# One DMA queue, a new order of the first chunks' transfers, and weight conversions spread anew in a fused RWKV-7 and GELU MLP kernel

## The chip, the cores and the metric

The kernel runs on one core of one Trainium2 chip. A core has five engines with queues of their own: TensorE (PE, with its weight loads shown apart as PEld), VectorE (DVE), ScalarE (ACT), GpSimd (POOL) and SyncE (SP), which here only issues transfers. Each engine works through its instructions in order and waits on semaphores for the others. The metric is device time in microseconds (us), the median of several runs.

## The reference, cut to what matters

A recurrence over 768 steps runs for 4 batches of 8 heads with a 40 x 40 state; its output, seen as 3072 tokens of 320 values, goes through an MLP with an exact GELU. The two weights arrive as 64-bit floats (an array of `float32` times a numpy scalar of 64 bits), so a kernel has to make 32-bit floats of them.

```python
for t in range(S):                                  # S = 768
    y[:, :, t] = np.einsum('bhd,bhde->bhe', rt, state)
    Sa = np.einsum('bhde,bhe->bhd', state, at)
    state_decay = state * wt[:, :, None, :] - np.einsum('bhd,bhe->bhde', Sa, bt)
    state = state_decay + np.einsum('bhd,bhe->bhde', vt, kt)
x = y.transpose(0, 2, 1, 3).reshape(3072, 320)
h = x @ w_in                                        # 320 x 2048
g = 0.5 * h * (1.0 + erf(h * inv_sqrt2))
out = g @ w_out                                     # 2048 x 320
```

## The kernel before

The 768 steps are cut into 12 chunks of 64. In a chunk the recurrence becomes matrix products: with the running products of the decay w (`logs`, `sums`), b, k and a are scaled (`scale_b`, `scale_k`, `scale_a`) and flipped (`turn_*`); masked products of them give N, A, RV and M. The triangular system with N is inverted in blocks of 32 by 31 column steps on VectorE or GpSimd. N goes to HBM and comes back spread over partitions for that, and the inverse takes the same way back. Its corner is joined by products on TensorE (`corner`, `joined`: J). From it come `sa`, then QY, the outputs and the next state. The MLP of a chunk is cut into eight pieces, which `fill()` puts between the steps of later chunks: four make `ph` and the Gelu, four make `po`.

Chunks 0, 1 and 2 and the conversion of both weights are written out one after the other; the later chunks run in a loop. The parts that matter here, with cuts:

```python
    def rows_of ... / def fetch(c, n, src, eng, t=None):   # two transfers of 64 x 16 x 40
        ...
    def scale_k(c, eng=nc.gpsimd):
        rwv, _ = decays.pop(c)
        ks = turned_in[c]["ks"] = ks_ring()
        eng.tensor_tensor(ks[:, :, :, :D], raws.pop((c, "k")), rwv, ALU.mult)

    def to_float(dst, words, eng):                  # one piece: 64-bit words to 32-bit floats
        ...
        nc.vector.tensor_scalar(power, hi, 0x7FF00000, None, ALU.bitwise_and)
        nc.scalar.activation(power, power, ACT.Relu, bias=rebias, scale=8.0)
        nc.vector.tensor_scalar(mant, hi, 0x000FFFFF, 0x00100000, ALU.bitwise_and, ALU.bitwise_or)
        if eng is nc.vector:
            yield                                   # the rest comes with the next piece
        nc.vector.scalar_tensor_tensor(power, hi, 0x80000000, power, ALU.bitwise_and, ALU.bitwise_or)
        if eng is nc.vector:
            eng.scalar_tensor_tensor(mant_f, lo, 2.0 ** -32, mant, ALU.mult, ALU.add)
            eng.scalar_tensor_tensor(dst, mant_f, 2.0 ** -20, power_f, ALU.mult, ALU.mult)
        else:                                       # GpSimd: two products on ScalarE, then
            nc.scalar.mul(lo_f, lo, 2.0 ** -52)
            nc.scalar.mul(mant_f, mant, 2.0 ** -20)
            eng.tensor_tensor(mant_f, mant_f, lo_f, ALU.add)
            eng.tensor_tensor(dst, mant_f, power_f, ALU.mult)
        yield

    def convert(n, last=False):                     # begin n pieces, end the one begun before each
        for _ in range(n):
            begun.append(queue.pop(0)); next(begun[-1], None)
            if len(begun) > 1: next(begun.pop(0), None)
        if last:
            while begun: next(begun.pop(0), None)

    def first_load(last, part, at=None): ...        # part of w_in, four transfers (eight if last)
    def second_load(f, slot, at=late_raw): ...      # row block f of w_out, into a slot of raw words
    def seconds(n, *loads, last=False):             # convert(n), then these second_loads

    def store_inverse(c, engs=(nc.sync,)): ...      # 2 transfers; engs takes turns
    def fetch_inverse(c, engs=(nc.sync,)): ...      # 6 transfers, into Tt and T2
```

The raw words of the second weight lie in the tile that takes the result and in one spare tile, so a load into a slot waits until the block that was there has been read. The written-out part, cut to the steps that the change touches:

```python
    load_w(0); fetch(0, "b", ...); load_a(0); load_w(1, early_w); fetch(1, "b", ...); load_a(1, early_a)
    fetch(0, "k", k, nc.sync)
    fetch(1, "k", k, nc.sync, ahead["k"])
    # ... N of chunk 0 and 1, inverse of chunk 0 on VectorE, of chunk 1 on GpSimd
    load_VR(0); load_r(0); load_w(2)
    first_load(False, 0, early(0, 4)); first_load(False, 1)
    # ... products of chunk 0
    run(inverse)
    queues = nc.sync, nc.scalar
    store_inverse(0, queues); load_VR(1)
    first_pieces((0,), 0, nc.vector); convert(1)
    fetch_inverse(0, queues)
    mask_A(0); mask_RV(0); make_av(0); make_A(1, False)
    # ... joined(0) to outputs(0), the same of chunk 1, the rest of the first weight
    second_pieces(range(NF), nc.vector)             # NF = 16
    seconds(2); fill(); turn_k(2); seconds(1); fill()
    make_QY(1); outputs(1); pieces.append(mlp(1))
    turn_v(2); turn_r(2); make_RV(2); make_A(2)
    load_w(3); load_kb(3); load_VR(3); load_a(3)
    seconds(6); fill(); seconds(0, (10, 12))
    make_av(2); logs(3); sums(3); scale(3)
    # ... seconds(1), (1), (2), (1), (2) with the loads of blocks 11 to 15 between
    for c in range(2, NCH): ...                     # the loop
```

Of the kernel before, what the change touches and what calls it, by code (L numbers as in the profile page):

```python
# [12 lines left out]
ALU = mybir.AluOpType  # L13
# [6 lines left out]
def kernel(  # L20
# [119 lines left out]
    def fetch(c, n, src, eng, t=None):  # L140
        if t is None:
            t = work.tile([P, G, H, D], FP32, tag=n + "_raw", name=n + "_raw")
        for e in range(2):
            eng.dma_start(out=t[half(e)].rearrange("p g h d -> p (g h) d")[:, :, :D], in_=rows_of(src, c, e))
        raws[c, n] = t
# [24 lines left out]
    def load_w(c, t=None, eng=nc.sync):  # L170
        t = w_tile if t is None else t
        fetch(c, "w", w, eng, t[:, :G * DM].rearrange("p (g h d) -> p g h d", g=G, h=H))
        raws[c, "w"] = t
# [14 lines left out]
    def load_VR(c):  # L188
        VR = turned_in.setdefault(c, {})["VR"] = VR_ring()
        for e in range(2):  # L190
            nc.sync.dma_start(out=VR[half(e)].rearrange("p g q m d -> p (g q m) d")[:, :, :D], in_=rows_of(v, c, e))
# [34 lines left out]
    load_w(1, early_w)  # L226
    fetch(1, "b", b, nc.sync, ahead["b"])
    load_a(1, early_a)
    fetch(0, "k", k, nc.sync)
    fetch(1, "k", k, nc.sync, ahead["k"])  # L230
    for t in (paired["a"], early_a):
        nc.gpsimd.memset(by_64(t)[:, :, D:], 0.0)

# [75 lines left out]
    def convert(n, last=False):  # L309

        for _ in range(n):
            begun.append(queue.pop(0))
            next(begun[-1], None)
            if len(begun) > 1:
                next(begun.pop(0), None)
        if last:
            while begun:
                next(begun.pop(0), None)
# [56 lines left out]
    def first_pieces(kts, part, eng):  # L375
        queue.extend(first_convert(kt, part, eng) for kt in kts)
# [4 lines left out]
    def run(steps):  # L381
        for _ in steps:
            pass
# [4 lines left out]
    def logs(c):  # L388
        logw = raws[c, "w"][:, :G * DM]
        nc.scalar.activation(logw, logw, ACT.Ln)  # L390
# [43 lines left out]
    def scale_b(c):  # L434
        rwv, wp = decays[c]
        nb = nb_ring()
        nc.vector.scalar_tensor_tensor(nb[:, :, :, :D], raws.pop((c, "b")), -1.0, rwv, ALU.mult, ALU.mult)
        turned_in.setdefault(c, {}).update(nb=nb, wp=wp)
# [5 lines that stand above are left out]
# [29 lines left out]
    def turn_k(c):  # L473
        t = turned_in[c]
        kT = side("kT", "kT", 1)
        nc.scalar.copy(kT, flip(by_pair(t["ks"]), "kT_ps"))  # L476
        t["kT"] = parts(kT)
# [93 lines left out]
    def make_av(c):  # L571
        t = turned_in[c]
        av = duo("av")[:, :, :G * NP * D].rearrange("p x (g i d) -> p x g i d", g=G, i=NP)
        for g, i, x, e, q, m in units():
            mm(av[half(e ^ x), x, g, i], t["A"][half(e), x, g, i], t["VR"][half(e), g, q, m, :D])
        avs = t["avs"] = avs_ring()
        nc.scalar.copy(avs[:, :, :DM], av.rearrange("p x g i d -> p x (g i d)"))
# [4 lines left out]
    def start_inverse(c, eng, place=None):  # L582

        n = P // 2
        blk = blocks.pop(c).rearrange("j z n s t -> (j z n) s t")
        if place is None:
            Nb = work.tile([P, BL * BL], FP32, tag="Nb", name="Nb")
            W = work.tile([P, BL // 2 * BL], FP32, tag="W", name="W")
            tmp = work.tile([P, BL * BL // 7], FP32, tag="tmp", name="tmp")
        else:  # L590
            Nb, W, tmp = place
        Nb, W = (t.rearrange("p (s t) -> p s t", t=BL) for t in (Nb, W))
        eng.memset(W, 0.0)  # L593
        for par in range(2):
            nc.sync.dma_start(out=Nb[par * n:(par + 1) * n], in_=blk)
            eng.memset(W[par * n:(par + 1) * n].rearrange("p s t -> p (s t)")[:, par::BL + 2][:, :BL // 2], 1.0)
        inverses[c] = W

        def columns():
            for j in range(BL - 1):  # L600
                rows, rest = j // 2 + 1, BL - 1 - j
                t = tmp[:, :rows * rest].rearrange("p (s t) -> p s t", s=rows)
                views = [W[:, :rows, j:j + 1].to_broadcast([P, rows, rest]),
                         Nb[:, j:j + 1, j + 1:].to_broadcast([P, rows, rest]), W[:, :rows, j + 1:]]
                if eng is nc.vector and rest < rows:

                    t = tmp[:, :rows * rest].rearrange("p (t s) -> p t s", s=rows)
                    views = [u.rearrange("p s t -> p t s") for u in views]
                eng.tensor_tensor(t, views[0], views[1], ALU.mult)  # L609
                eng.tensor_tensor(views[2], views[2], t, ALU.add)  # L610
                yield
        return columns()

# [2 lines left out]
    def store_inverse(c, engs=(nc.sync,)):  # L616
        W = inverses[c]
        n = P // 2
        inv = dram.tile([2, 2, 2 * G * NP, BL, BL], FP32, tag="inv", name="inv")
        rows = inv.rearrange("j z n (s q) t -> q (j z n) s t", q=2)  # L620
        for par in range(2):
            engs[par % len(engs)].dma_start(out=rows[par], in_=W[par * n:(par + 1) * n])
        stored[c] = inv

    def fetch_inverse(c, engs=(nc.sync,)):
        inv = stored.pop(c)
        Tt = Tt_ring()
        T2 = work.tile([P, G * NP, BL], FP32, tag="T2", name="T2")
        for z in range(2):
            for j in range(2):  # L630
                at = j * HP + z * BL
                engs[j % len(engs)].dma_start(out=flat(Tt)[at:at + BL, :, z * BL:(z + 1) * BL],
                                              in_=inv[j, z].rearrange("n s t -> s n t"))
        for j in range(2):

            engs[j % len(engs)].dma_start(out=T2[j * HP:j * HP + BL],
                                          in_=inv[j, 1].rearrange("(n z) s t -> z s n t", z=2)[1])
        inverses[c] = Tt, T2
# [199 lines left out]
    def early(n, k=1):  # L838

        at = late_raw if n < NK else scratch  # L840
        return at[:, n % NK * LW:(n % NK + k) * LW]
# [19 lines left out]
    make_N(0)  # L861
    logs(1)
    sums(1)
    scale_k(0)
    inverse = start_inverse(0, nc.vector)
    scale_b(1)
    turn_a(1)
    scale_a(1)
    warm(3)
    turn_b(1)  # L870
    scale_k(1)
    make_N(1)

    spare_x = work.tile([P, NK, TB], FP32, tag="xt", name="spare_x").rearrange("p k t -> p (k t)")
# [2 lines left out]
    spare_w = spare_st.rearrange("p e i g d -> p (e i g d)")  # L877
    nw = BL // 2 * BL
    run(start_inverse(1, nc.gpsimd, (spare_x[:, :BL * BL], spare_w[:, :nw], spare_w[:, nw:])))
    load_VR(0)  # L880
    load_r(0)
    load_w(2)
    first_load(False, 0, early(0, 4))
    first_load(False, 1)
    turn_k(0)
# [1 line left out]
    turn_v(0)  # L887
    turn_r(0)
    make_RV(0, False)
    turn_k(1)  # L890
    logs(2)
    run(inverse)
    queues = nc.sync, nc.scalar
    store_inverse(0, queues)
    load_VR(1)
    first_pieces((0,), 0, nc.vector)
    convert(1)
    fetch_inverse(0, queues)
    mask_A(0)
    mask_RV(0)  # L900
    make_av(0)
    make_A(1, False)
    first_load(True, 0, early(4))
    load_r(1)
    first_load(False, 2, early(5, 4))
    convert(0, True)
    mask_A(1)
    corner(0)
    joined(0)
    first_pieces((1, 2), 0, nc.gpsimd)  # L910
# [7 lines left out]
    make_y2(0)  # L918
    make_M(0)
    store_inverse(1)  # L920
    load_a(2)
    fetch(2, "b", b, nc.sync)
    fetch_inverse(1)
    first_load(False, 3)
    nc.gpsimd.memset(spare_st.rearrange("p e i g d -> p (e i g) d")[:, :, D:], 0.0)
    convert(2, True)
    make_QY(0)
    outputs(0)
    pieces.append(mlp(0))
    make_av(1)  # L930
    corner(1)
    turn_v(1)
    turn_r(1)
    joined(1)
    turn_state()
    make_X(1)
    make_RV(1)
    for f in range(2):
        second_load(f, 2 * f)
# [3 lines left out]
        second_load(f, 2 * f)  # L943

    first_pieces(range(NK), 1, nc.gpsimd)
    sums(2)
    convert(1)
    make_sa(1)
# [4 lines left out]
    convert(1)  # L953
    fill()
    turn_b(2)
    convert(1)
    fill()
    scale_k(2)
    make_N(2)
    convert(1)  # L960
    make_y2(1)
    make_M(1)
    convert(1, True)
    for n in "av":
        unused(paired[n], nc.gpsimd)
    run(start_inverse(2, nc.gpsimd))
# [3 lines left out]
    second_load(9, 2, spare_raw)  # L970

    second_pieces(range(NF), nc.vector)
    seconds(2)
    fill()
    turn_k(2)
    seconds(1)
    fill()
    make_QY(1)
    outputs(1)
    pieces.append(mlp(1))  # L980
# [1 line left out]
    turn_r(2)  # L982
    make_RV(2)
    make_A(2)
    load_w(3)
    load_kb(3)
    load_VR(3)
    unused(paired["r"], nc.vector)
    load_a(3)
    seconds(6)  # L990
    fill()
    seconds(0, (10, 12))
    make_av(2)
    logs(3)
    sums(3)
    scale(3)
    turn_a(3)
    scale_a(3)
    turn_state()
    seconds(1, (11, 14))  # L1000
    fill()
    seconds(1, (12, 0, spare_raw), (13, 2, spare_raw))
    turn_b(3)
    store_inverse(2)
    fetch_inverse(2)
    seconds(2, (14, 14))
    seconds(1, (15, 0, spare_raw))
    load_r(3)
    load_v(3)
# [95 lines left out]
```

## Time and profile before

| | |
|---|---|
| time | 781.34 us, median of 3 runs (781.34 to 783.16) |
| span of the profiled run | 776.1 us |
| granted TensorE clock, mean | 0.942 |
| TensorE busy | 701.0 us, 90% |
| weight loads, VectorE, ScalarE, GpSimd busy | 561.1, 273.7, 220.0, 313.0 us |
| moved by DMA | 67.82 MB, 87 GB/s |

An "L" and a number give the line of the kernel that an instruction comes from: L290 to L304 are the conversion, L609 and L610 the column steps of the inverse, L796 the MLP's first product, L804 its second, L100 the helper for the small products. What an engine waited for is shown with an arrow. A busy TensorE is not one at its peak: its clock may be throttled, which is shown as granted clock, 1.00 being all of it. Times of a stage say more here than those of the whole, as the written-out start and the loop have different limits.

### The profile page before, as it was taken

What the parts mean: (1) busy time and instruction counts of PE and PEld (TensorE: products, weight loads), DVE (VectorE), ACT (ScalarE), POOL (GpSimd) and SP (SyncE); (2) the same over time, 40 slices, a digit from 0 to 9 for tenths busy, and PEclk for the clock granted to TensorE, in tenths of its full rate; (3) what the DMA queues carried; (4) which work ended last, traced back from release to release, by engine and by line L of the source; (5) the groups of instructions that cost most, each with busy time, mean ns of one, the idle gap of its engine ahead of it and who ended that gap; (6) DMA issues with size and microseconds to landing.
All of it is one profiled execution on the core that took longest, in us unless ns stands there. A gap on an engine that the chain in (4) does not pass through costs nothing.

```text
span 776.1 us, 30554 instructions
## 1 busy us (share of the span) xinstructions
PE 701.0 (90%) x13792; PEld 561.1 (72%) x13792; DVE 273.7 (35%) x419; ACT 220.0 (28%) x262; POOL 313.0 (40%) x779
## 2 busy tenths in 40 slices
PE   7346786675999999999999999999999999999997
PEld 5336675442887887887877877878878878778685
DVE  3677354746234124143143242242341241321100
ACT  5134363242232332241331342322322313112020
POOL 4385158810381471570750842822814805600000
PEclk9666897867999999999999999999999999999999
DMA  9887655536633724725635536436337241120100
GB/s 137 132 156 138 141 156 99 82 65 150 126 69 66 142 56 77 140 46 95 118 64 105 98 67 119 87 67 120 76 69 141 55 74 38 25 45 3 26 9 17
DMA packets 268361, 67.82 MB, mean 87 GB/s; under 512 B 256616, under 2 KB 261512, under 8 KB 268232
## 3 DMA queue, kind: packets, MB, share of 16 engines
q1 hardware_dynamic: 265664, 65.41, 44.8%
q8 instruction: 108, 1.77, 0.9%
q10 hardware_dynamic: 2568, 0.46, 0.3%
q14 instruction: 21, 0.17, 0.1%
HBM read 51.68 MB, written 10.22 MB: 80 GB/s over the span
## 4 chain that ended last, share of the span: by engine, by line
PE 81%; DVE 4%; DMA 4%; issue 4%; SPq 3%; POOL 2%; ACT 1%; POOLq 0%; DVEq 0%; ACTq 0%
PE ph L796 27%; PE po L804 26%; PE QY L100 6%; PE J L100 2%; PE av L100 2%; PE sap L100 2%; PE cum L100 2%; PE saT_ps L100 2%; PE N_ps L100 2%; DMA w_out_sb<-in_moe_w_in_dram 1%; PE RV_ps L100 1%; PE X L100 1%; PE A_ps L100 1%; PE kT_ps L415 1%; PE nT_ps L415 1%
## 5 line engine op out<-in xcount | busy, mean ns | idle before, releaser
L804 PE MATMUL po<-w_out_sb,gt 128*128 128x320 f32 x768 | 225.0, 445 | 18.9 <-DVE w_out_sb L299 17.2
L796 PE MATMUL ph<-xt,w_in_sb 64*128 64x256 f32 x1920 | 223.9, 385 | 6.3 <-POOL w_in_sb L304 6.1
L796 PEld LDWEIGHTS ph<-xt,w_in_sb 64*128 64x128 f32 x1920 | 184.8, 189 | 30.3 <-POOL w_in_sb L304 7.3
L804 PEld LDWEIGHTS po<-w_out_sb,gt 128*128 128x128 f32 x768 | 143.1, 193 | 83.7 <-DVE w_out_sb L299 26.1
L609 POOL TENSOR_TENSOR tmp<-W,Nb 128x126 f32<-128x126 f32 (+22 forms) x310 | 113.2, 365 | 171.1 <-DMA Nb<-N 147.6
L610 POOL TENSOR_TENSOR W<-W,tmp 128x126 f32<-128x126 f32 (+22 forms) x310 | 116.5, 376 | 24.3
L798 ACT ACTIVATE gt<-ph 128x1024 f32<-128x1024 f32 x48 | 49.2, 1026 | 169.2 <-PE ph L796 169.1
L808 DVE COPY os<-po 128x320 f32<-128x320 f32 x24 | 11.8, 492 | 107.9 <-PE po L804 107.9
L509 DVE TENSOR_TENSOR SM<-M_ps,upper 128x1024 f32<-128x1024 f32 x12 | 14.7, 1223 | 67.7 <-PE M_ps L100 67.7
L753 DVE TENSOR_TENSOR xt<-QY,wpT 128x512 f32<-128x512 f32 x24 | 15.5, 686 | 60.6 <-PE QY L100 60.6
L593 POOL MEMSET W<- 128x512 f32 x10 | 5.3, 531 | 73.5 <-DMA inv<-W 73.4
L675 DVE COPY Tt<-J 32x512 f32<-32x512 f32 x12 | 8.3, 688 | 73.7 <-ACT Tt L675 73.7
L476 ACT COPY kT<-kT_ps 128x1024 f32<-128x1024 f32 x12 | 12.2, 1014 | 65.9 <-PE kT_ps L415 65.9
L443 POOL TENSOR_TENSOR ks<-k_raw,part 128x640 f32<-128x640 f32 x10 | 16.2, 1618 | 36.4 <-ACT part L405 26.7
L509 DVE TENSOR_TENSOR A<-A_ps,upper 128x1024 f32<-128x1024 f32 x12 | 14.7, 1223 | 40.9 <-PE A_ps L100 40.9
L509 DVE TENSOR_TENSOR VR<-RV_ps,upper 128x1024 f32<-128x1024 f32 x12 | 14.7, 1224 | 40.8 <-PE RV_ps L100 40.8
L291 ACT ACTIVATE power<-power,rebias 128x320 uint32<-128x320 uint32 (+1 forms) x26 | 16.3, 627 | 42.9 <-DVE power L290 42.9
L100 PEld LDWEIGHTS av<-VR,A 64*64 64x64 f32 x768 | 14.1, 149 | 15.1 <-issue 15.1
L798 ACT ACT_TABLE_LOAD x10 | 12.8, 1283 | 42.6 <-PE ph L796 42.5
L100 PE MATMUL av<-VR,A 64*64 64x40 f32 x768 | 15.6, 240 | 10.0 <-DVE A L509 9.5
L100 PEld LDWEIGHTS QY<-SM,nb 64*64 64x64 f32 x768 | 18.7, 140 | 5.1 <-issue 3.6
L100 PE MATMUL QY<-SM,nb 64*64 64x104 f32 x768 | 21.2, 262 | 1.3 <-DVE SM L509 1.3
(152 smaller groups left out, 870.8 us busy)
## 6 DMA issues: line engine op xcount, KB each, us to landing
Nb<-N SPq DMA_DIRECT2D x22, 256.0 KB
VR<-in_v_dram SPq DMA_DIRECT2D x24, 160.0 KB
out_dram<-os SPq DMA_DIRECT2D x48, 80.0 KB
w_tile<-in_w_dram SPq DMA_DIRECT2D x22, 160.0 KB
b_raw<-in_b_dram SPq DMA_DIRECT2D x22, 160.0 KB
k_raw<-in_k_dram SPq DMA_DIRECT2D x22, 160.0 KB
w_out_sb<-in_moe_w_out_dram SPq DMA_DIRECT2D x11, 320.0 KB
N<-N SPq DMA_DIRECT2D x48, 64.0 KB
```

The lines of the kernel that those rows point to most:

```text
L100: nc.tensor.matmul(o, lhsT, rhs, start=first, stop=True, skip_group_check=True)
L291: nc.scalar.activation(power, power, ACT.Relu, bias=rebias, scale=8.0)
L415: nc.tensor.transpose(pt[:, g, n], src(g, n), ident)
L443: eng.tensor_tensor(ks[:, :, :, :D], raws.pop((c, "k")), rwv, ALU.mult)
L476: nc.scalar.copy(kT, flip(by_pair(t["ks"]), "kT_ps"))
L509: nc.vector.tensor_tensor(to, pt, upper.unsqueeze(1).to_broadcast([P, 2 * G * NP, C]), ALU.mult)
L609: eng.tensor_tensor(t, views[0], views[1], ALU.mult)
L610: eng.tensor_tensor(views[2], views[2], t, ALU.add)
L753: nc.vector.tensor_tensor(xt[:, :NP, g * P:(g + 1) * P].rearrange("p i (e t) -> p i e t", e=2), Y, wp[:, g, :, :, :C], ALU.mult)
L796: nc.tensor.matmul(ph[:, x, s], w_in_sb[half(x), kt, p * P:(p + 1) * P], xt[half(x), kt], start=kt == 0, stop=kt == NK - 1)
L798: nc.scalar.activation(gt[:, 4 * q:4 * q + 4].rearrange("p (x s) t -> p x s t", x=2), ph, ACT.Gelu)
L804: nc.tensor.matmul(po[:, g], gt[:, f, g * P:(g + 1) * P], w_out_sb[:, f], start=f == 0, stop=f == NF - 1)
```

## The change

It orders the start of the kernel anew. The two k's are no longer loaded with the other first inputs: that of chunk 0 follows the fetch of N of chunk 0, that of chunk 1 the fetch of N of chunk 1, and the scaling of the second goes to VectorE. w of chunk 2 moves behind the store of the inverse of chunk 0, and this store and its fetch go through SyncE's queue alone. The fetch of the inverse of chunk 1 goes ahead of a and b of chunk 2, and r of chunk 1 right ahead of it. In chunk 1 the flips of v and r come behind X. The conversions of the first weight are spread so that fewer stand ahead of the outputs of chunk 0 and one more stands ahead of the sums of chunk 2; the scaling of k of chunk 2 comes after them. The conversions of the second weight go 3, 3, 2, 1, 1, 1, 2, 1, 2 rather than 2, 1, 6, 1, 1, 2, 1, 2, with their loads between, and the logarithm of w of chunk 3 ahead of the product av of chunk 2. Last, VectorE's column steps use one form of views for all columns. It is for shorter waits before the loop begins.

```diff
@@ -226,8 +226,6 @@
     load_w(1, early_w)
     fetch(1, "b", b, nc.sync, ahead["b"])
     load_a(1, early_a)
-    fetch(0, "k", k, nc.sync)
-    fetch(1, "k", k, nc.sync, ahead["k"])
     for t in (paired["a"], early_a):
         nc.gpsimd.memset(by_64(t)[:, :, D:], 0.0)
 
@@ -600,14 +598,9 @@
             for j in range(BL - 1):
                 rows, rest = j // 2 + 1, BL - 1 - j
                 t = tmp[:, :rows * rest].rearrange("p (s t) -> p s t", s=rows)
-                views = [W[:, :rows, j:j + 1].to_broadcast([P, rows, rest]),
-                         Nb[:, j:j + 1, j + 1:].to_broadcast([P, rows, rest]), W[:, :rows, j + 1:]]
-                if eng is nc.vector and rest < rows:
-
-                    t = tmp[:, :rows * rest].rearrange("p (t s) -> p t s", s=rows)
-                    views = [u.rearrange("p s t -> p t s") for u in views]
-                eng.tensor_tensor(t, views[0], views[1], ALU.mult)
-                eng.tensor_tensor(views[2], views[2], t, ALU.add)
+                eng.tensor_tensor(t, W[:, :rows, j:j + 1].to_broadcast([P, rows, rest]),
+                                  Nb[:, j:j + 1, j + 1:].to_broadcast([P, rows, rest]), ALU.mult)
+                eng.tensor_tensor(W[:, :rows, j + 1:], W[:, :rows, j + 1:], t, ALU.add)
                 yield
         return columns()
 
@@ -861,14 +854,14 @@
     make_N(0)
     logs(1)
     sums(1)
-    scale_k(0)
     inverse = start_inverse(0, nc.vector)
+    fetch(0, "k", k, nc.sync)
     scale_b(1)
     turn_a(1)
     scale_a(1)
     warm(3)
     turn_b(1)
-    scale_k(1)
+    scale_k(0)
     make_N(1)
 
     spare_x = work.tile([P, NK, TB], FP32, tag="xt", name="spare_x").rearrange("p k t -> p (k t)")
@@ -877,9 +870,9 @@
     spare_w = spare_st.rearrange("p e i g d -> p (e i g d)")
     nw = BL // 2 * BL
     run(start_inverse(1, nc.gpsimd, (spare_x[:, :BL * BL], spare_w[:, :nw], spare_w[:, nw:])))
+    fetch(1, "k", k, nc.sync, ahead["k"])
     load_VR(0)
     load_r(0)
-    load_w(2)
     first_load(False, 0, early(0, 4))
     first_load(False, 1)
     turn_k(0)
@@ -887,24 +880,23 @@
     turn_v(0)
     turn_r(0)
     make_RV(0, False)
-    turn_k(1)
-    logs(2)
     run(inverse)
-    queues = nc.sync, nc.scalar
-    store_inverse(0, queues)
+    store_inverse(0)
     load_VR(1)
-    first_pieces((0,), 0, nc.vector)
-    convert(1)
-    fetch_inverse(0, queues)
+    load_w(2)
+    fetch_inverse(0)
+    scale_k(1, nc.vector)
     mask_A(0)
     mask_RV(0)
     make_av(0)
+    turn_k(1)
     make_A(1, False)
+    first_pieces((0,), 0, nc.vector)
+    convert(1, True)
+    mask_A(1)
+    logs(2)
     first_load(True, 0, early(4))
-    load_r(1)
     first_load(False, 2, early(5, 4))
-    convert(0, True)
-    mask_A(1)
     corner(0)
     joined(0)
     first_pieces((1, 2), 0, nc.gpsimd)
@@ -918,22 +910,23 @@
     make_y2(0)
     make_M(0)
     store_inverse(1)
+    load_r(1)
+    fetch_inverse(1)
     load_a(2)
     fetch(2, "b", b, nc.sync)
-    fetch_inverse(1)
     first_load(False, 3)
-    nc.gpsimd.memset(spare_st.rearrange("p e i g d -> p (e i g) d")[:, :, D:], 0.0)
-    convert(2, True)
+    convert(1, True)
     make_QY(0)
     outputs(0)
     pieces.append(mlp(0))
     make_av(1)
     corner(1)
-    turn_v(1)
-    turn_r(1)
+    convert(1, True)
     joined(1)
     turn_state()
     make_X(1)
+    turn_v(1)
+    turn_r(1)
     make_RV(1)
     for f in range(2):
         second_load(f, 2 * f)
@@ -943,6 +936,7 @@
         second_load(f, 2 * f)
 
     first_pieces(range(NK), 1, nc.gpsimd)
+    convert(1)
     sums(2)
     convert(1)
     make_sa(1)
@@ -953,14 +947,14 @@
     convert(1)
     fill()
     turn_b(2)
-    convert(1)
     fill()
-    scale_k(2)
     make_N(2)
     convert(1)
     make_y2(1)
     make_M(1)
     convert(1, True)
+    scale_k(2)
+    nc.gpsimd.memset(spare_st.rearrange("p e i g d -> p (e i g) d")[:, :, D:], 0.0)
     for n in "av":
         unused(paired[n], nc.gpsimd)
     run(start_inverse(2, nc.gpsimd))
@@ -970,11 +964,11 @@
     second_load(9, 2, spare_raw)
 
     second_pieces(range(NF), nc.vector)
-    seconds(2)
+    seconds(3)
     fill()
     turn_k(2)
-    seconds(1)
     fill()
+    seconds(3)
     make_QY(1)
     outputs(1)
     pieces.append(mlp(1))
@@ -982,28 +976,29 @@
     turn_r(2)
     make_RV(2)
     make_A(2)
+    unused(paired["r"], nc.vector)
     load_w(3)
-    load_kb(3)
+    fetch(3, "b", b, nc.sync)
+    seconds(2, (10, 12))
+    logs(3)
+    fetch(3, "k", k, nc.sync)
     load_VR(3)
-    unused(paired["r"], nc.vector)
     load_a(3)
-    seconds(6)
+    seconds(1, (11, 14))
     fill()
-    seconds(0, (10, 12))
+    seconds(1, (12, 0, spare_raw))
+    seconds(1, (13, 2, spare_raw))
     make_av(2)
-    logs(3)
     sums(3)
     scale(3)
     turn_a(3)
     scale_a(3)
     turn_state()
-    seconds(1, (11, 14))
     fill()
-    seconds(1, (12, 0, spare_raw), (13, 2, spare_raw))
+    seconds(2, (14, 14))
     turn_b(3)
     store_inverse(2)
     fetch_inverse(2)
-    seconds(2, (14, 14))
     seconds(1, (15, 0, spare_raw))
     load_r(3)
     load_v(3)
```

## The prediction

> **What bounds the kernel now.** I read the page's slices first, then the busy time by stage, then TensorE's timeline in the stages that have gaps, and last VectorE's timeline and the waits there. By stage (columns: stretch, busy time of TensorE, its weight loads, VectorE, ScalarE and GpSimd with their counts, granted clock, DMA share, GB/s):
>
> ```profile
> 0.00:40.00 40.00, 22.90 (x411) 16.89 (x411) 19.90 (x54) 13.71 (x15) 16.32 (x52) 0.83 0.91 135
> 40.00:80.00 40.00, 20.33 (x719) 18.37 (x718) 30.65 (x49) 14.90 (x22) 27.47 (x54) 0.70 0.79 147
> 80.00:120.00 40.00, 31.52 (x802) 27.10 (x804) 19.01 (x26) 20.42 (x28) 12.35 (x9) 0.90 0.53 138
> 120.00:140.00 20.00, 17.23 (x238) 13.71 (x239) 7.61 (x18) 5.36 (x8) 16.46 (x39) 0.78 0.47 90
> 140.00:160.00 20.00, 11.14 (x150) 5.53 (x148) 17.46 (x37) 5.26 (x8) 13.84 (x33) 0.74 0.77 123
> 160.00:180.00 20.00, 15.51 (x172) 10.68 (x172) 10.18 (x23) 9.85 (x12) 2.20 (x1) 0.75 0.25 63
> 180.00:202.00 22.00, 14.20 (x138) 8.88 (x140) 11.06 (x24) 2.71 (x4) 0.78 (x3) 0.69 0.54 114
> 202.00:776.00 574.00, 568.16 (x11190) 459.95 (x11176) 157.82 (x195) 147.75 (x167) 223.58 (x590) 1.00 0.40 75
> ```
>
> After 202 us TensorE is busy 568.16 of 574.00 us, in a loop that the change leaves alone. Before 202 us it idles 202 - 132.8 = 69 us. So only the first 202 us can give or take anything, and what they give comes off the end whole. From 140 to 202 us the holes are these (TensorE's timeline, then VectorE's; start, duration, what ended the idle time before):
>
> ```profile
> 143.96 1.34 PE L804 MATMUL po<-w_out_sb,gt 128*128 128x320 f32 x4
> 149.21 1.20 PE L804 MATMUL po<-w_out_sb,gt 128*128 128x320 f32 x2 [3.90 <-DVE w_out_sb L299]
> 160.17 1.44 PE L804 MATMUL po<-w_out_sb,gt 128*128 128x320 f32 x2 [0.49 <-DVE w_out_sb L299]
> 161.53 1.95 PE L100 MATMUL av<-VR,A 64*64 64x40 f32 x64
> 166.34 2.50 PE L100 MATMUL cum<-w_tile,cum_m 128*128 128x320 f32 x4 [2.86 <-ACT w_tile L390]
> 188.93 1.44 PE L804 MATMUL po<-w_out_sb,gt 128*128 128x320 f32 x2 [5.62 <-DVE w_out_sb L299]
> ```
>
> ```profile
> 127.57 0.49 DVE L299 SCALAR_TENSOR_TENSOR w_out_sb<-mant,power 128x320 f32<-128x320 f32 x1
> 137.80 1.29 DVE L753 TENSOR_TENSOR xt<-QY,wpT 128x512 f32<-128x512 f32 x2 [9.73 <-PE QY L100]
> 169.62 0.82 DVE L437 SCALAR_TENSOR_TENSOR nb<-b_raw,part 128x640 f32<-128x640 f32 x1 [9.50 <-ACT part L405]
> 186.98 0.33 DVE L290 TENSOR_SCALAR power<-w_out_sb 128x320 uint32<-128x320 uint32 x1 [4.53 <-DMA w_out_sb<-in_moe_w_out_dram]
> ```
>
> VectorE converts the 16 row blocks of the second weight, two by 128 us; then it stands still for 9.73 us, and TensorE afterwards waits for blocks 2 to 7 one by one until 161.6 us. It stands still again for 9.50 us before 169.62, and at 186.98 waits for the load of a block which could only be issued once a slot had been read.
>
> **What the Trainium skill says.** "SBUF — State Buffer", section "Who interferes with whom": VectorE and GpSimd share a port pair, and VectorE instructions with two SBUF inputs block against GpSimd reads. The trace agrees: one conversion step takes 146.52 to 149.19 = 2.67 us beside GpSimd's inverse, 172.87 to 174.78 = 1.91 us without it. "DMA: Bandwidth & Descriptors", section "Issuing engines are not separate DMA queues": a second issuing engine saves issue time only. In the trace the inverse of chunk 0 is stored from both queues at 48.86 and lands at about 53.24, when the next issue on SyncE gets through; so I charge the single queue little. "TensorE: Matmul & The Clock Gate", section "What's actually happening": an idle array is throttled. Granted clock here: 0.69 to 0.78 from 120 to 202 us and 1.00 afterwards.
>
> **The change, part by part.**
>
> *(1) The k's leave the front of the queue.* N of chunk 0 is ready at 14.21 + 1.22 = 15.4 us, but its store is issued only at 17.23, behind both k's. Now it goes at once, and its fetch before k. VectorE's inverse then starts no longer with the fetch (26.39) but behind the mask of N of chunk 1 (22.52 + 1.23 = 23.75): about 2.4 us earlier. It takes 48.84 - 26.39 = 22.45 us, so it ends near 46.4. The plain view in place of the turned one for the last ten columns I count as nothing: 31 elements in one row take 0.19 us, 126 in six rows 0.29, the slope of one element per cycle without a visible cost per row.
>
> *(2) What that is worth is mostly lost in the queue.* Up to 51.46 us VectorE's first weight conversion waits for DMA, and the DMA share is 0.91. By then the queue has moved the same bytes as it will in the changed kernel between the store of N of chunk 1 and the last first-weight piece (k of chunk 1 takes the place of w of chunk 2), so I leave 51.4 us. The store of the inverse lies behind those pieces, lands near 53, and its fetch now has v of chunk 1 and w of chunk 2 ahead of it: 2 x 0.33 MB at about 145 GB/s = 4.5 us, part of it in what is now an empty gap. The masks of A and RV leave earlier (near 47.1 to 49.5 rather than 52.42), but TensorE's J needs the fetch: near 60 us against 60.29 now. Sum of (1) and (2): 0, give or take 2.
>
> *(3) Chunk 1 and the first weight, 72 to 123.6 us.* One conversion (kt 3) instead of two lies between the mask of M and xt, so xt starts with QY's end (76.0) and not at 78.53. J2 and X of chunk 1 go ahead of the flips of v and r. Against that, ScalarE's three conversion steps (0.72 + 0.69 + 0.62 us) delay the copy into Tt. I carry 1.3 us to the RV mask (93.12 now). Then the first second-half piece starts ahead of the cumulative sum's exponentials, and k of chunk 2 (113.30, 1.55 us on GpSimd) no longer sits between the last pieces. Chaining VectorE 0.8, ScalarE 2.0 and GpSimd 2.6 us per piece, with the last two still behind the masks of N and M, the last first-weight tile is done at 120.5 and not 123.6 (122.32 + 1.26): 3 us.
>
> *(4) The second weight, 120 to 162 us.* Three conversions are begun before the third MLP piece and three more before QY. ScalarE runs in order, so the exponents of blocks 3 to 5 wait for the fourth Gelu (135.00 + 1.03, less 3 = 133.0). Block 4 is therefore done near 137 and xt of chunk 1 starts there, against 137.80. So five blocks are done where two were. The A mask ends at 142.8 (145.5 now), the two memsets at 143.7; then the ends of blocks 5, 6 and 7 at 2.2 us each: 150.3, and the last matmuls 1.4: 151.7 against 161.6. That is 9.9 us, of which 3 are from (3); new: 6.9.
>
> *(5) logs of chunk 3 ahead of av.* cum waits 2.86 us for ScalarE at 166.34, because the logarithm is behind the copy of av. With the new order the w load (issued about 146, landed about 150) and the logarithm are done before av ends (153.6). New: 2.8 us. cum is then at 153.7, against 166.34: 12.6 us.
>
> *(6) Blocks 8 to 15.* Blocks 8 and 9 are done before that; a of chunk 3 lands near 159 and VectorE turns and scales it until 161.6. Four loads are now issued at 149 to 158, not 157.69 to 176.5. Block 14's load goes once block 11 is read, 165; then the store and fetch of the inverse, 8 us (176.18 to 183.97 now), then block 15's load at 173.3, landed 3 us later, and two steps: 180.5. Now the same piece ends at 193.6: 13 us. Nothing new, nothing lost.
>
> Sum: 0 + 3 + 6.9 + 2.8 = 12.7 us off 781.34: 768.6, say **769 us**.
>
> **The rivals.** *The start loses.* One queue and w of chunk 2 ahead of the fetch could put J of chunk 0 3 to 5 us later, as the DMA share of 0.91 suggests; SyncE's many waits for free semaphores speak for it too. Against it: the DMA share between 52 and 54 us is 0.03, a gap that the new order fills. It would leave 772 to 775. *A transfer takes over at the end.* Parts (4) and (5) could be hidden by block 15's load, which sits behind the store and fetch of the inverse. If k, v and a of chunk 3 land later than I have it, every step of (6) slips and the kernel ends at 774 to 779. The 4.53 us wait at 186.98 speaks for it; but the waits that hold that load are for earlier conversions, and those move. *More is gained.* A busier TensorE keeps its clock: 0.72 on average over 140 to 202 us leaves about 10 us of slowness to recover, and the pieces of (3) could pack closer. That would make 758 to 763. *Slower*, by more than 2% (797), would need 16 us of new waits, for which I find no place.
>
> **Range and chances.** The upstream shift is uncertain by 3 us, block conversions by 3, the last loads by 4: together about 6, and the first two rivals pull more ways than the third. Range 760 to 777. 2% is 765.7, which needs 15.6 us, three more than the sum: chance 0.32. Within 2%: 0.64. Slower: 0.04.
>
> **What would show it.** Right: VectorE's inverse of chunk 0 starts near 24; J of chunk 0 within 2 us of 60; the last first-weight tile near 120.5; five blocks of the second weight done before xt of chunk 1; no wait of cum for w at 154; the 20-matmul rhythm without idle from about 189 us on instead of 202. Wrong: J later than 63; block 7 after 156; a DMA wait of over 6 us ahead of block 15; or a loop after 202 us that is no longer at 99% busy.

## The result, and the profile after

The changed kernel takes 769.82 us, median of 4 runs (767.67 to 771.25), against 781.34 us: a ratio of 0.9848, 95% interval 0.9814 to 0.9882. The prediction was 769.0. Measured once more later, beside its own runs of the kernel before, it took 773.99 us (767.53 to 775.71, ratio 0.9913, interval 0.9880 to 0.9946). The ten executions together have a median of 772, so the gain is about 9 us, with a spread between executions (767.5 to 775.7) that is nearly as wide. That lies in the predicted range of 760 to 777, on the side of less than 2% to which the prediction gave 0.64.

The changed kernel by stage, in the columns of the prediction's table:

```profile
0.00:40.00 40.00, 24.24 (x408) 17.95 (x408) 22.11 (x55) 13.32 (x14) 16.30 (x56) 0.80 0.89 128
40.00:80.00 40.00, 21.86 (x786) 19.70 (x784) 30.49 (x50) 13.42 (x20) 22.72 (x46) 0.69 0.79 148
80.00:120.00 40.00, 30.93 (x744) 25.74 (x746) 18.96 (x27) 23.06 (x33) 17.03 (x13) 0.95 0.66 161
120.00:140.00 20.00, 17.49 (x367) 15.03 (x364) 16.41 (x32) 7.44 (x10) 17.15 (x41) 0.93 0.34 63
140.00:160.00 20.00, 15.28 (x161) 9.76 (x162) 15.33 (x30) 9.15 (x12) 15.02 (x32) 0.75 0.87 154
160.00:180.00 20.00, 9.43 (x33) 5.37 (x32) 12.21 (x29) 3.71 (x6) 0.77 (x3) 0.76 0.46 102
180.00:202.00 22.00, 22.00 (x360) 17.04 (x361) 6.21 (x9) 4.15 (x5) 6.46 (x20) 0.83 0.66 126
202.00:776.00 574.00, 557.98 (x10944) 450.73 (x10940) 156.09 (x192) 144.42 (x163) 216.02 (x570) 1.00 0.38 72
```

The last row ends with the kernel, at 765.9 us: TensorE is busy all but some 6 us of it, as before. Between 180 and 202 us it no longer idles (22.00 of 22.00 against 14.20). From 120 to 140 us VectorE works 16.41 us where it worked 7.61: those are the conversions of the second weight that were moved ahead. But between 160 and 180 us TensorE now works 9.43 us, against 15.51. A hole has been moved forward and has not gone.

TensorE's timeline of the changed kernel (start, duration, what ended the idle time before):

```profile
60.12 1.08 PE L100 MATMUL J<-L,N 32*32 32x32 f32 x64 [3.54 <-DVE L L638]
...
119.16 4.55 PE L789 MATMUL ph<-xt,w_in_sb 64*128 64x256 f32 x24 [3.14 <-POOL w_in_sb L302]
139.79 4.65 PE L797 MATMUL po<-w_out_sb,gt 128*128 128x320 f32 x10
...
150.77 1.44 PE L797 MATMUL po<-w_out_sb,gt 128*128 128x320 f32 x2 [1.78 <-DVE w_out_sb L297]
152.14 1.95 PE L100 MATMUL av<-VR,A 64*64 64x40 f32 x64
154.02 2.50 PE L100 MATMUL cum<-w_tile,cum_m 128*128 128x320 f32 x4
...
179.50 2.76 PE L797 MATMUL po<-w_out_sb,gt 128*128 128x320 f32 x4 [6.71 <-DVE w_out_sb L297]
...
182.20 1.99 PE L100 MATMUL N_ps<-aT,nT 40*64 40x64 f32 x64
```

J of chunk 0 begins where it did (60.12, 60.29 before). Ten matmuls at 139.79 are five row blocks in one go, as step (4) had it; cum follows av at once, as step (5) had it. The next piece then waits 6.71 us for its last block. VectorE's timeline shows for what:

```profile
24.13 0.19 DVE L601 TENSOR_TENSOR tmp<-W,Nb 128x31 f32<-128x31 f32 x1 [0.74 <-DMA Nb<-N]
...
25.54 0.22 DVE L601 TENSOR_TENSOR tmp<-W,Nb 128x56 f32<-128x56 f32 x1
25.79 1.43 DVE L603 TENSOR_TENSOR W<-W,tmp 128x56 f32<-128x56 f32 x1
...
48.09 0.19 DVE L603 TENSOR_TENSOR W<-W,tmp 128x16 f32<-128x16 f32 x1
...
160.64 1.25 DVE L167 STREAM_TRANSPOSE aT<-a_pairs 128x1024 f32<-128x1024 f32 x1 [2.53 <-DMA a_pairs<-in_a_dram]
161.99 1.23 DVE L456 TENSOR_TENSOR aT<-aT,wpT 128x1024 f32<-128x1024 f32 x1
...
177.56 0.33 DVE L288 TENSOR_SCALAR power<-spare_raw 128x320 uint32<-128x320 uint32 x1 [6.26 <-DMA spare_raw<-in_moe_w_out_dram]
```

Late in the stage VectorE waits for two transfers: for a of chunk 3 at 160.64, and for block 15 at 177.56. The experiments are about these, and about what a part of the change is worth alone.

Three measures are used below, because they compare kernels whose earlier stages end at different times. *Start* is the time at which J of chunk 0 begins. *Middle* runs from there to the tile group that waited for the last tile of the first weight (119.16 above: 59.0 us). *Second* runs from there to the product N of chunk 3, which follows the last block of the second weight (182.20 - 119.16 = 63.0 us). The kernel before has 60.29, 63.3 and 69.9, from these lines:

```profile
60.29 1.08 PE L100 MATMUL J<-L,N 32*32 32x32 f32 x64 [1.97 <-DVE L L645]
...
123.63 5.49 PE L796 MATMUL ph<-xt,w_in_sb 64*128 64x256 f32 x24 [2.61 <-POOL w_in_sb L304]
...
193.55 1.99 PE L100 MATMUL N_ps<-aT,nT 40*64 40x64 f32 x64
```

In the tables these stages, and the clocks, come from one profiled execution of each kernel; the time is the median of all its executions. The two need not match: the profiled execution of *changed again* took 767.53 us, the fastest of six with a median of 773.99.

### The profile page after: what moved, and what is told of

Read it like the earlier page. It is cut to its first block, busy times and chain, and to the rows that moved or that the text cites. A ratio compares the mean times of both kernels' runs of the same rounds, so it can differ in the third digit from the quotient of the medians.

```text
span 765.9 us, 30557 instructions
## 1 busy us (share of the span) xinstructions
PE 699.2 (91%) x13792; PEld 561.3 (73%) x13792; DVE 277.8 (36%) x420; ACT 218.7 (29%) x262; POOL 311.5 (41%) x778
## 4 chain that ended last, share of the span: by engine, by line
PE 77%; POOL 7%; SPq 5%; issue 5%; DMA 4%; DVE 1%; ACT 0%; POOLq 0%; DVEq 0%; ACTq 0%
PE po L797 26%; PE ph L789 26%; PE QY L100 5%; PE J L100 2%; PE N_ps L100 2%; POOL tmp L601 1%; POOL W L603 1%; PE sap L100 1%; PE X L100 1%; DMA a_pairs<-in_a_dram 1%; POOL st L603 1%; PE saT_ps L100 1%; PE kT_ps L413 1%; PE nT_ps L413 1%; PE cum L100 1%
## 5 line engine op out<-in xcount | busy, mean ns | idle before, releaser
L601 POOL TENSOR_TENSOR tmp<-W,Nb 128x126 f32<-128x126 f32 (+22 forms) x310 | 111.6, 360 | 172.8 <-DMA Nb<-N 149.2
L603 POOL TENSOR_TENSOR W<-W,tmp 128x126 f32<-128x126 f32 (+22 forms) x310 | 118.6, 383 | 24.3
L575 ACT COPY avs<-av 128x640 f32<-128x640 f32 x12 | 8.3, 693 | 53.5 <-PE av L100 53.5
```

The source lines that it names most:

```text
L601: eng.tensor_tensor(t, W[:, :rows, j:j + 1].to_broadcast([P, rows, rest]), Nb[:, j:j + 1, j + 1:].to_broadcast([P, rows, rest]), ALU.mult)
L603: eng.tensor_tensor(W[:, :rows, j + 1:], W[:, :rows, j + 1:], t, ALU.add)
```

## The experiments

**First round: each part alone, and one load moved.** The change falls into three parts that can be applied singly: the start (queue, k's, plain views; steps 1 and 2), the middle (conversions of the first weight and chunk 1's order; step 3) and the second weight (steps 4 to 6). The core of each, against the kernel before:

```diff
 # start only
-    fetch(0, "k", k, nc.sync)                 # both k's ahead of N
-    fetch(1, "k", k, nc.sync, ahead["k"])
+    fetch(0, "k", k, nc.sync)                 # behind start_inverse(0)
+    fetch(1, "k", k, nc.sync, ahead["k"])     # behind start_inverse(1)
-    store_inverse(0, queues)
+    store_inverse(0)
 # ... plain views in the column steps, w of chunk 2 behind v of chunk 1, scale_k(1) on VectorE,
 # ... first piece of the first weight and logs(2) behind A of chunk 1
```

> The kernel before with the new start alone (up to the first corner). Theory A (the start nets nothing, as the queue takes back what the earlier inverse gives): VectorE's inverse of chunk 0 starts near 24.1, J of chunk 0 at 60 give or take 1, end at 781 give or take 2. Rival B (the earlier inverse and the single queue carry part of the gain): J of chunk 0 at 57 to 58, end at 776 to 779. Rival C (the start loses, later parts make up for it): J at 62 or later, end above 783.

```diff
 # middle only
-    convert(2, True)
+    convert(1, True)
     make_QY(0)
 # ...
-    turn_v(1)
-    turn_r(1)
+    convert(1, True)
     joined(1)
     turn_state()
     make_X(1)
+    turn_v(1)
+    turn_r(1)
 # ... r of chunk 1, the memset and scale_k(2) later, one conversion ahead of sums(2)
```

> The kernel before with the new order from the first corner to the last conversion of the first weight alone. Theory A: last first-weight tile released near 119 to 120 (123.6 before), everything after it about 4 us earlier, end at 777. Rival (the loads of the last row blocks take the place of what is removed): end at 780 to 782.

```diff
 # second weight only
-    seconds(2)
+    seconds(3)
     fill()
     turn_k(2)
-    seconds(1)
     fill()
+    seconds(3)
 # ... the rest of the second weight's lines in the diff of the change
```

> The kernel before with the new spread of the second weight's conversions and of chunk 3's loads alone. Theory A: the fifth MLP piece ends near 156.7 (161.6 before), cum of chunk 3 near 158.5 (166.3 before), of which about 2 us are lost again by the late clock and loads: end at 775. Rival (needs the middle's shift to be of use; block 15's load sets the end): 779 to 781.

The fourth kernel is the changed one with the load of block 15 ahead of the inverse's way through HBM:

```diff
+    seconds(1, (15, 0, spare_raw))
     store_inverse(2)
     fetch_inverse(2)
-    seconds(1, (15, 0, spare_raw))
```

> The changed kernel with the load of row block 15 ahead of the store and fetch of chunk 2's inverse. Theory A (this load is the last wait in front of the loop): VectorE's wait of 6.26 us at 177.56 shrinks to under 1, the seventh piece ends near 176, end at 764 (769.8 now). Rival (the fetch of the inverse or the clock takes its place at once): end at 768 to 770.

| kernel | start | middle | second | time, us | ratio, 95% interval |
|---|---|---|---|---|---|
| before | 60.29 | 63.3 | 69.9 | 780.04 | 1 |
| start only | 60.95 | 65.0 | 69.7 | 781.03 | 1.0019 (1.0000 to 1.0037) |
| middle only | 59.27 | 61.6 | 70.7 | 779.51 | 0.9991 (0.9975 to 1.0008) |
| second only | 58.87 | 64.0 | 63.5 | 772.65 | 0.9916 (0.9894 to 0.9938) |
| changed, block 15 first | 61.07 | 66.8 | 56.5 | 767.81 | 0.9846 (0.9808 to 0.9884) |

The second weight's part brings most of the gain. The start brings nothing. The middle's tile is released at 120.90 and not 123.63, near the 119 to 120 that was expected, but the time, 779.51, stays near the 780 to 782 of its rival. The load of block 15 is what the last piece waited for. SyncE's issues in the changed kernel:

```profile
166.45 0.33 SPq L367 DMA_DIRECT2D w_out_sb<-in_moe_w_out_dram  x1
166.87 1.28 SPq L615 DMA_DIRECT2D inv<-W  x2
170.94 1.93 SPq L625 DMA_DIRECT2D Tt<-inv  x4
172.91 0.98 SPq L629 DMA_DIRECT2D T<-inv  x2
173.93 0.45 SPq L367 DMA_DIRECT2D spare_raw<-in_moe_w_out_dram  x1
```

The fetch (170.94) can only go when the store (166.87) has landed, and the load behind it in the same queue stands still as well, until 173.93. With the load ahead of the store, SyncE issues in this order:

```profile
176.60 0.33 SPq L367 DMA_DIRECT2D spare_raw<-in_moe_w_out_dram  x1
177.03 1.28 SPq L615 DMA_DIRECT2D inv<-W  x2
```

and TensorE's last piece of that kernel reads:

```profile
181.63 2.76 PE L797 MATMUL po<-w_out_sb,gt 128*128 128x320 f32 x4 [0.52 <-DVE w_out_sb L297]
```

The piece's wait falls from 6.71 to 0.52 us and the stage from 63.0 to 56.5. Yet the time of 767.81 us is not clearly under the changed kernel's. Its middle stage is the reason: 66.8 us instead of 59.0, though up to about 165 us this kernel has the same instructions in the same order. So the stage's length has another cause too. The stretches 60 to 80 and 80 to 100 us (TensorE's granted clock is the third column from the right), of the changed kernel:

```profile
60.00:80.00 20.00, 14.15 (x576) 13.10 (x576) 14.82 (x21) 7.05 (x13) 5.78 (x7) 0.71 0.72 137
80.00:100.00 20.00, 16.68 (x464) 14.18 (x466) 10.03 (x15) 12.71 (x19) 8.22 (x6) 0.91 0.63 147
```

and of this one:

```profile
60.00:80.00 20.00, 14.35 (x440) 13.21 (x444) 12.00 (x16) 6.25 (x11) 7.08 (x12) 0.50 0.66 130
80.00:100.00 20.00, 16.07 (x484) 14.03 (x479) 7.65 (x14) 7.33 (x11) 2.56 (x2) 0.73 0.73 152
```

The clock was 0.71 and 0.91 in one execution, 0.50 and 0.73 in the other. The same products take longer in the second. The flip of v of chunk 1, in the changed kernel at a clock of 1.00 (82 to 86 us) and in this one at 0.50 (90 to 94 us):

```profile
83.12 1.97 PE L100 MATMUL vT_ps<-ident,VR 128*64 128x128 f32 x32
```

```profile
90.24 3.68 PE L100 MATMUL vT_ps<-ident,VR 128*64 128x128 f32 x32
```

Up to about 67 us this kernel runs a steady 0.9 us behind the changed one (VectorE's copy of `sap` begins at 67.12 and 66.18). From 68 to 70 us the granted clock is 0.96 in the changed kernel and 0.50 in this one, and from there the lag grows, to 9.0 us at the product RV of chunk 1 (96.22 and 87.22). So in these two executions the lower clock came first and the longer stage after it, some 8 us in a chain where the other engines wait for TensorE. Why the clock differed is not shown. From here on stages are compared at like clocks where there are such.

**Second round: one part undone, and the changed kernel again.** Each of these is the changed kernel with one part as it was before (the diffs above, turned round).

> The changed kernel with the start of before (both k's in front, two queues, w of chunk 2 early). Theory A (the start nets nothing by itself): within 1.5 us of the changed kernel on the same chip. Rival (the start is worth something together with the middle, as the three parts alone summed to 6 us against 11.9 for the whole): 3 to 5 us slower than the changed kernel.

> The changed kernel with before's order from the first corner to the last conversion of the first weight. Theory A as predicted (the middle is worth 3 to 4.5 us): 3 to 4.5 us slower than the changed kernel. Rival (the middle is worth little, as alone in the kernel before: 0.7 us): 0 to 2 us slower; the earlier RV mask of the first profile was the clock of one execution.

> The changed kernel with before's spread of the second weight. Theory A: 7 us slower than the changed kernel, near 777. Rival (the parts help each other, the second weight is worth more on top of the others): 9 to 11 us slower, near 780.

> The changed kernel as it is, on the chip of the three runs above, for their comparison. Theory A: ratio to before 0.985 as measured first, about 769. Rival (the first four runs were lucky in TensorE's clock): ratio 0.989 to 0.992, 772 to 774, which is what the three parts alone sum to.

| kernel | start | middle (clock 60-80, 80-100) | second | time, us | ratio, 95% interval |
|---|---|---|---|---|---|
| start undone | 60.71 | 62.0 (0.58, 0.83) | 63.8 | 770.25 | 0.9863 (0.9835 to 0.9891) |
| middle undone | 60.82 | 65.1 (0.58, 0.91) | 64.2 | 774.42 | 0.9933 (0.9910 to 0.9956) |
| second undone | 60.05 | 61.0 (0.61, 0.83) | 70.7 | 778.83 | 0.9979 (0.9962 to 0.9996) |
| changed again | 59.33 | 57.9 (0.73, 1.00) | 63.4 | 773.99 | 0.9913 (0.9880 to 0.9946) |

Start: undoing it costs nothing. At 770.25 us the kernel is even 3.7 us under *changed again*, which neither expectation had; the intervals overlap (0.9835 to 0.9891 and 0.9880 to 0.9946), so a small cost of the new start is neither shown nor excluded. Middle: at a clock of about 0.6 and then 0.83, the new order takes 61.0 to 62.0 us (here, and 61.6 where it was alone; 62.9 in a kernel of the third round), the old one 64.0 to 65.0 (second only at 0.65, 0.83; start only at 0.59, 0.83). That is 1 to 4 us, about 3; the first profile's 4.3 came at an unlike clock (0.71, 0.91 against 0.73, 0.83). Second: 63.4 to 64.2 us with the new order, 70.7 without. In the times the middle is worth 0.1 to 0.5% (middle alone against before; start undone against second only), the second weight 0.7 to 1.3% (changed again against second undone; start undone against middle only). On the one chip of this round, undoing the middle costs 0.4 us, as the rival expected, and undoing the second weight 4.8, less than either expectation; *changed again* came out as its rival had it.

The 22 executions of the kernel with the second part undone also show that time goes with the clock: at a mean granted clock of 0.942 it took 772.74 us, at 0.929 about 781 (the five at that clock lie between 779.3 and 782.9); over all 22 the correlation is -0.84 and the slope 5.7 us for 0.01. One kernel on one chip thus spreads over 10 us.

**Third round: steps (4), (5) and (6) apart, the clock, and all together.** The logs of chunk 3 back behind av:

```diff
     seconds(2, (10, 12))
-    logs(3)
     fetch(3, "k", k, nc.sync)
 # ...
     make_av(2)
+    logs(3)
     sums(3)
```

> The changed kernel with the logarithm of chunk 3's w behind the product av again. Theory A as predicted (part 5 is worth 2.8 us): cum of chunk 3 starts 4.8 us after av rather than 1.9, and the stage from the last first-weight tile to N of chunk 3 takes 66 us, not 63.4. Rival (block 15's load sets the end of that stage, so the gain of part 5 is hidden): cum later by 2.9, the stage 63 to 64.5 us.

The second weight's first conversions as they were before, the rest as in the changed kernel:

```diff
-    seconds(3)
+    seconds(2)
     fill()
     turn_k(2)
     fill()
-    seconds(3)
+    seconds(1)
     make_QY(1)
 # ...
-    seconds(2, (10, 12))
+    seconds(5, (10, 12))
```

> The changed kernel with 2, 1 and then 5 conversions of the second weight in place of 3, 3 and 2: VectorE's idle stretch ahead of QY is left empty again. Theory A (filling it is what shortens the fifth MLP piece): from the last first-weight tile to av of chunk 2 about 38 us, not 33, and the stage to N of chunk 3 about 67 to 68. Rival (block 15's load hides it): 38 us to av, but 63 to 65 for the stage.

The changed kernel with products that nobody reads in the gaps of TensorE (two of 128 x 384 ahead of the corner of chunk 0, one ahead of that of chunk 1, and one of 128 x 256 behind saT of chunk 0):

```diff
-    corner(0)
+    corner(0, (3, 3))        # products into the unused half of J's tile
 # ...
     make_saT(0)
+    warm(2)
 # ...
-    corner(1)
+    corner(1, (3,))
```

> The changed kernel with a few products of two constants, whose result nobody reads, in TensorE's gaps ahead of J of chunk 0, M of chunk 0 and J of chunk 1. Theory C (the spread of some 8 us between executions of the changed kernel is the granted clock between 60 and 100 us): clock from 60 to 100 us at 0.85 or more in every profile, the stage from J of chunk 0 to the last first-weight tile 57 to 59 us, times near 767 with a small spread. Rival (the gaps are too short to matter, or the added products cost what they give): clock 0.5 to 0.7 from 60 to 80, times 768 to 775 as without.

And a kernel that keeps those products, loads block 15 ahead of the store, loads a of chunk 3 right behind b, and begins three, two and one conversions where the change begins three and three:

```diff
     turn_k(2)
+    seconds(2)
     fill()
-    seconds(3)
+    seconds(1)
     make_QY(1)
 # ...
     fetch(3, "b", b, nc.sync)
+    load_a(3)
     seconds(2, (10, 12))
 # ...
-    load_a(3)
 # ...
+    seconds(1, (15, 0, spare_raw))
     store_inverse(2)
     fetch_inverse(2)
-    seconds(1, (15, 0, spare_raw))
```

> The changed kernel with these products, block 15's load ahead of the inverse's store, the exponents of blocks 3 and 4 ahead of the fourth Gelu (conversions 3, 2, 1), and a of chunk 3 loaded before k and v. Theory A: the stage from the last first-weight tile to N of chunk 3 takes 53 us (63.4 in the changed kernel, 56.5 with the load alone), end at 757 to 760. Rival (the moves meet a common limit, for example VectorE's conversions): the stage stays at 56 us, end at 763 to 766.

| kernel | middle (clock) | last first-weight tile to av | av to cum | second | time, us | ratio, 95% interval |
|---|---|---|---|---|---|---|
| before | 63.3 (0.73, 0.83) | 37.9 | 4.8 | 69.9 | 780.24 | 1 |
| changed (first profile) | 59.0 (0.71, 0.91) | 33.0 | 1.9 | 63.0 | 769.82 | 0.9848 (0.9814 to 0.9882) |
| logs late | 62.9 (0.62, 0.81) | 33.0 | 4.9 | 63.6 | 774.78 | 0.9927 (0.9901 to 0.9953) |
| two, one, five | 64.2 (0.54, 0.83) | 38.3 | 1.9 | 67.3 | 776.21 | 0.9948 (0.9928 to 0.9968) |
| idle products | 59.0 (0.71, 0.91) | 33.0 | 1.9 | 64.6 | 769.13 | 0.9877 (0.9846 to 0.9908) |
| all moves | 60.2 (0.68, 1.00) | 32.6 | 1.9 | 54.0 | 760.10 | 0.9746 (0.9716 to 0.9776) |

(Ratios are to the kernel before in the same round; the time of before shown is that of the third.)

*Logs late*: cum follows av 4.9 us behind and not 1.9, and the stage is as long as ever: 63.6 against 63.0 to 64.2. VectorE shows why:

```profile
163.80 0.82 DVE L435 SCALAR_TENSOR_TENSOR nb<-b_raw,part 128x640 f32<-128x640 f32 x1 [5.03 <-ACT part L403]
164.54 1.24 DVE L167 STREAM_TRANSPOSE aT<-a_pairs 128x1024 f32<-128x1024 f32 x1
```

The step behind cum now waits 5.03 us, and the turn of a, which had waited 2.53 us for its transfer, waits for nothing. In both kernels it begins between 41 and 42 us behind the last first-weight tile. The earlier logs only exchange one wait for another.

*Two, one, five*: without the early conversions av comes 5.3 us later, and the stage is 67.3 us instead of about 63.5. So step (4) is real, and some 4 of its 5 us come through to the end of the stage.

*Idle products*: the clock in its profile is the same as in the first profile of the changed kernel, four of six executions lie between 768.1 and 769.7 and the others at 772.1 and 774.8. That suggests a steadier clock and doesn't show it; the intervals of the two kernels overlap.

*All moves*: VectorE's turn of a,

```profile
159.96 1.25 DVE L167 STREAM_TRANSPOSE aT<-a_pairs 128x1024 f32<-128x1024 f32 x1
```

and TensorE's timeline at the two ends of the stage:

```profile
121.43 5.49 PE L792 MATMUL ph<-xt,w_in_sb 64*128 64x256 f32 x24 [3.20 <-POOL w_in_sb L302]
...
172.76 2.77 PE L800 MATMUL po<-w_out_sb,gt 128*128 128x320 f32 x4 [1.23 <-DVE w_out_sb L297]
```

The turn no longer waits for its transfer and comes 159.96 - 121.43 = 38.5 us behind the last first-weight tile, against 41.5 in the changed kernel. The stage is 54.0 us: 6.5 of the gain were there with block 15's load alone. There the turn of a still came 168.88 - 127.83 = 41.05 us behind the tile, so it now comes 2.5 us earlier, which is what the stage gains besides. That points to a's earlier load, but the finer spread came with it, and the two were not tried apart. At 760.10 us this kernel is clearly faster than the changed one and than that with block 15's load alone.

## Why the prediction was right, and where its steps were not

The time was right, and so in the main was the mechanism: the gain lies in the second weight, with a smaller share from the middle and none from the start. Several sizes were off, in part hidden by a good clock in the first executions; the step that failed is (6).

**(1) and (2), the start: sum right, (1) mis-sized.** VectorE's inverse begins at 24.13, as predicted (about 24), though what it waits for at the end is still the fetch of N (0.74 us) and not the mask. But it takes 48.28 - 24.13 = 24.15 us and not 22.45, so it ends 0.6 us earlier than before and not 2.4. The k's have moved, and GpSimd's product with k, which ran ahead of the inverse before, now runs beside it:

```profile
25.62 1.53 POOL L441 TENSOR_TENSOR ks<-k_raw,part 128x640 f32<-128x640 f32 x1 [17.20 <-DMA k_raw<-in_k_dram]
```

The VectorE step at 25.79 takes 1.43 us; its neighbour of the same size takes 0.22. This is the blocking that the prediction took from the Trainium skill, "SBUF — State Buffer", section "Who interferes with whom", and applied to the conversions only. It explains 1.2 of the 1.7 us. Most of the rest is in the steps of 128 to 121 elements, which now fall deeper into GpSimd's own column steps for chunk 1: they take 39.14 - 34.05 = 5.09 us, against 39.77 - 35.10 = 4.67 before. As step (2) says that an earlier end is lost in the queue, the sum stayed 0. No cost of the plain views is seen: the last part of the inverse, from the first turned step on, takes 48.84 - 39.77 = 9.07 us before and 48.28 - 39.14 = 9.14 after. But both run beside GpSimd's column steps, which may hide a small cost. The single queue was not tried apart. With the rest of the start it nets nothing or a little less (start only is at 1.0019, with J at 60.95). That fits the Trainium skill, "DMA: Bandwidth & Descriptors", section "Issuing engines are not separate DMA queues", by which a second issuing engine saves only issue time, but it does not show it apart.

**(3), the middle: right.** 3 us predicted, about 3 measured at like clocks. The flips no longer stand in the way: the second part of J of chunk 1 begins 1.3 us behind the first (79.07 and 80.34), where it was 6.5 us (81.66 and 88.14). It is hardly seen in the time where it stands alone (0.9991): in its profile the second stage is 0.8 us longer and what comes behind it 1.7 us (584.2 against 582.6), for reasons that the runs don't show.

**(4), the second weight's early blocks: mechanism right, term mis-sized.** Five blocks were done ahead, as predicted. The stretch from the last first-weight tile to av shrank by 37.9 - 33.0 = 4.9 us, where the prediction had 6.9. Most of the rest is pace: blocks 5 to 7 take 2.71, 2.74 and 2.55 us beside GpSimd's inverse, and not 2.2. The prediction had such a step at 2.67 us in its own reading of the trace before, and charged less.

**(5), the logs: confirmed in the trace, worth nothing in the time.** cum does come 2.9 us earlier behind av (4.8 to 1.9). The late-logs kernel shows that the wait for a takes its place, so these 2.8 us of the sum were lost.

**(6), "Nothing new, nothing lost": this step failed.** The prediction put the landing of a at 159, with the turn and scaling done at 161.6, that is 41.1 us behind its last first-weight tile (120.5). Measured, they end at 161.99 + 1.23 = 163.2, which is 44.1 us behind it (119.16): 3 us later. SyncE issues a's load at 152.75, behind w and b of chunk 3, a weight block, and k and v. What follows keeps a lag of 2 to 3 us: the load of block 14 that waits for block 11 (2.8 us), the load of block 15 (2.0), the end of the last piece (3.1). The stage is 63.0 us where the prediction's own times give 180.5 - 120.5 = 60.0. The second rival had named this, and it took back about 3 us of the 12.7. These 3 us and the 2.8 of (5) are one loss and not two, since the wait for a is what took the earlier cum's place. That a's load is the cause rests on this chain and on the last kernel above, where a is loaded ahead of k and v, nothing waits for it, and the turn begins 38.5 us behind the tile, as the prediction had it (159 - 120.5). Block 15's load behind the inverse was priced about rightly (8 us predicted, 166.45 to 173.93 measured), but taken as given: the fourth kernel shows that the order of three lines was worth 6.5 us of the stage.

**The sum.** With the sizes measured: 0 for the start, about 3 for the middle, about 6.5 for the second stage, less about 1 behind it (583.7 us from N of chunk 3 to the end, 582.6 before), makes some 8 to 9 us and not 12.7, or about 773 us. The median of all ten executions is 772. The first four, at 769.82, were better than this, and their clock was better too (a mean of 0.944, against 0.941 in the later six). So it was in part luck that the first time fell within 1 us of 769: the third rival's clock seems to have made up for what the second took. The Trainium skill, "TensorE: Matmul & The Clock Gate", section "What's actually happening", says that an idle array is throttled and that the window runs freely, so that one kernel can differ from run to run; it puts the ramp at under 1% of a typical span. Here executions of the unchanged instructions differ by up to 1.1% (767.5 to 775.7), in a kernel that has gaps in its stages up to 202 us. In the two profiles compared above the products took longer at the lower clock; what sets the clock in one execution and not in the other is not settled by these runs, and idle products in the gaps did not decide it.

## What to carry to other kernels

When a wait is taken away, ask which transfer is waited for next: in an in-order queue of transfers, a load that is needed soon should not stand behind a fetch that waits for a store to land. Judge an order of work stage by stage at like clocks, and take the time from many executions, since a stage with gaps can drift by more than its new order is worth (8.9 us against about 3 in the middle stage here). And moving a transfer also moves the engine work behind it, so look at what that work will now run beside.

## What the hardware showed that was not expected

- A two-input VectorE operation of 56 elements took 1.43 us instead of 0.22 beside one GpSimd product of 1.53 us and ended with it (27.22 and 27.15): moved by 7.5 us, a single GpSimd instruction delayed VectorE by 1.2 us.
- The same instructions took 57.9 to 66.8 us in the middle stage, with granted clocks from 0.73 and 1.00 down to 0.50 and 0.73.
- Beside GpSimd's column steps, VectorE's steps with rows of 1 to 10 elements took no longer than the same elements in longer rows (9.14 against 9.07 us for the last part of the inverse).
